# A retuned transformer block: first modulation in channel halves, first norm's inverse root on ScalarE

## The chip, the cores and the metric

The kernel runs as one program on one core of a Trainium2 chip. The metric is device time in microseconds (us). A core has five instruction streams that run side by side and meet only at semaphores: PE (TensorE, matmuls), ACT (ScalarE), DVE (VectorE), POOL (GpSimd) and SP (SyncE, which here only issues DMAs). A DMA is issued in an instant or, where its queue is full, in a few us, and lands much later.

## The reference

One block of an adaptive-layer-norm transformer, with 2048 tokens, 512 channels, 32 heads of 16 and a hidden width of 1792:

```python
mod = (silu(c) @ w_mod).reshape(1, 6, 1, 512)          # sa, ca, ga, sb, cb, gb
h = layernorm(x) * (1 + ca) + sa
q, k, v = split(h @ wqkv)                              # 32 heads of 16
# each token attends to itself and 7 earlier tokens, 2 apart
logits[s, w] = q[s] . k[s - 2 * w] * 16 ** -0.5        # w = 0..7, masked below token 0
x = x + ga * (softmax(logits) @ v) @ wo
h = layernorm(x) * (1 + cb) + sb
x = x + gb * ((gelu(h @ w_gate) * (h @ w_up)) @ w_down)
```

Shift `sa` and scale `1 + ca` are the first 1024 of the 3072 columns of `silu(c) @ w_mod`. Every channel of the first normalized activation needs its own two numbers from there, so the first q, k and v product waits for x, for c and for these columns.

## The kernel before, in words

Tokens go through in five groups (`GROUPS`): two of 256, then three of 512. For each group `ln1` (L567) normalizes rows, transposes them on PE and modulates them into `hT`; `emit_qkv` (L609) multiplies by wq, wk, wv and stores v to a scratch in DRAM; `emit_attention` (L657) reads v back as `vR`, forms the products on DVE (`pq`, `pv`), folds them on PE and ends in the output projection, the second norm and `h2T`; `emit_ffn` (L832) does gate, up and down products.

The order of instructions on each engine is not the order of the code. Every piece of work is an `Op` with an engine, an estimated duration and a priority; `Plan.order` (L92) places, again and again, the piece that could start earliest (start plus `MARGIN` of its engine), and among equals the one with the lowest priority number. `PRI`, `MARGIN`, `AHEAD` and `SKEW` (L200 to L219) are the knobs of that list. On the chip each engine then runs its list strictly in order. For loads: those with a priority under -996.9 are placed as soon as SP is free, the others no earlier than `AHEAD` us before the planned end of the transfers already issued. Buffers of one tag and sequence must be begun in the order in which they were made: x goes into `xs` in order, `wm2` can be loaded only after the tile `wide`, which needs `silu(c)`, has been placed, and the `qkv_ps` accumulators of group 0 come before those of group 1.

The first group, step by step. SP issues x of tokens 0 to 255 (L366), then `wm01`, the 1024 shift and scale columns, as one load with 2048 bytes in a row (L403), then wq, wk (L406), x of tokens 256 to 511, wv, more x. PE begins with 12 matmuls on zeros (L430), turns c into a column (L441) and does 4 more on zeros; ACT applies silu (L446). DVE takes the statistics of x (L578, L580), adds epsilon (L582); POOL raises to the power -1/2 (L513); DVE normalizes (L508); PE transposes both 128-token blocks (L553). `mod_first` (L469) multiplies `wm01` with silu(c) on PE, channel block 0 first and then blocks 1 to 3, both shift and scale, and adds 1 to the scale with a further one-column matmul (L483). DVE reads those numbers straight from PSUM to modulate the four channel blocks of `hT` (L561). q and k of the first half of the heads start block by block as `hT` arrives; order for this group: q, k, q, k, v, v. `mod_keep` (L489) copies shift and scale for the later groups. The other load names: `wm2` and `wm5` (gates ga, gb), `wm3` and `wm4` (shift and scale of the second norm), `woP`, `Wg`, `Wu`, `WdP`. `woP` and `WdP` are multiplied by the gates on DVE (L898, L901).

ACT holds one table of functions at a time. `emit` (L167) asks for the table with both exp and ln when the plan goes from a piece marked `silu` or `gelu` to one marked `exp`.

Of the kernel before, what the change touches and what calls it, by code (L numbers as in the profile page):

```python
# [184 lines left out]
class Engines:  # L185
    def __init__(self, nc, pl):
# [9 lines left out]
        ("rstd", 4), ("xn1", 2), ("xn2", 2), ("hT", 2), ("qT", 3), ("vT", 3), ("vR", 2), ("prod", 6), ("Lb", 1),  # L196
        ("e", 1), ("oT", 1), ("h2T", 2), ("gl", 3), ("ub", 3), ("hh", 8))
BLOCKS1 = ()
BLOCKS2 = ()
PRI = {  # L200
        "ln1": (-1549, -553.9, -424.8, -117.9, 420.6),
        "qkv": (-226.2, 479.5, 310.9, 823.2, 1490.9),
        "att": (-63.2, 258.1, -1202.2, 1315.4, 916.4),
        "ffn": (1214.3, 2234.3, 2417.5, 2391, 546),
        "glu": (-1006.6, 100.6, -1510.2, -71.4, 1415.7),
        "mod": (393, -373, -33.5),
        "wo": 1028.5,
        "wd": 1181.4,
        "scr": -3561.5,
        "vR": -3846.6,  # L210
        "warm": (12, 4, 0, 3),
        "load": {"wv": -989.49, "x1": -989.99, "x2": -962.38, "wm2": -989.49, "wo": -888.99, "x3": -991.49,
        "wm3": -899.52, "wm4": -990.99, "x4": -981.04, "Wg": -864.95, "Wu": -877.79, "wm5": -867.98, "Wd":
        -873.85},
}
Plan.MARGIN = {"pe": 0.34, "act": 1.25, "dve": 0.46, "pool": -1.19, "sp": 1.04}
Plan.AHEAD = 2.79
Plan.SKEW = 1.27
Plan.TURN = 0  # L219
# [3 lines left out]
def kernel(  # L223
# [13 lines left out]
    nc = tc.nc  # L237
# [44 lines left out]
    neghalf = ctile([P, 4], F32, "neghalf")  # L282
    onecol = ctile([P, 1], BF16, "onecol")
    M = ctile([P, H], BF16, "Mph")
    F1 = ctile([P, P], BF16, "F1")
# [23 lines left out]
    def consts_dve():  # L309
        nc.vector.memset(warm(), 0.0)  # L310
        nc.vector.memset(one1[:], 1.0)
        nc.vector.memset(neghalf[:], -0.5)
        nc.vector.memset(onecol[:], 1.0)

    def consts_ident():
# [27 lines left out]

    dve(0.6, consts_dve, w=[(early, 0), one1, neghalf, onecol], pri=-1000)
    gp(1.0, consts_ident, w=[ident], pri=-1000)
# [24 lines left out]

    wm01 = T("vR", [P, 4, 2 * D], BF16, "wm01", "early")
    wm3 = T("h2T", [P, 4, D], BF16, "wm3")
# [20 lines left out]
    def load_rows(t, src, p, cuts, late=0.0):  # L393
# [8 lines left out]
    load_x(0, 2, -1000)  # L402
    dma(1049e3, lambda: nc.sync.dma_start(out=wm01[:], in_=w_mod[:, 0:2 * D].rearrange("(t p) n -> p t n", p=P)),  # L403
        w=[wm01], pri=-999, bw=385e3)
    for b in range(3):
        dma(524e3, lambda b=b: nc.sync.dma_start(  # L406
            out=wqkv[b][:], in_=A_wqkv[:, b * D:(b + 1) * D].rearrange("(dt p) n -> p dt n", p=P)), w=[wqkv[b]],
            pri=(-998, -997, L["wv"])[b])
    load_x(2, 4, L["x1"])
# [58 lines left out]

    def mod_first(src, p):  # L469
        parts = []  # L470
        for chs in ((0,), (1, 2, 3)):
            n = len(chs)
            mps = T("psF", [P, 2 * n], F32, "modT_ps")

            def cols(chs=chs, n=n, mps=mps):
                for half in range(2):
                    for i, ch in enumerate(chs):
                        col = mps[:, half * n + i:half * n + i + 1]
                        for kt in range(4):
                            nc.tensor.matmul(col, lhsT=src[:, kt, half * D + ch * P:half * D + (ch + 1) * P],  # L480
                                             rhs=scT[:, kt:kt + 1], start=(kt == 0), stop=(kt == 3 and half == 0))
                        if half:
                            nc.tensor.matmul(col, lhsT=ident[:], rhs=onecol[:], start=False, stop=True)  # L483

            pe(0.25 * n, cols, r=[src, scT, ident, onecol], w=[mps], pri=p)
            parts.append((chs[0], n, mps))
        return parts

    def mod_keep(parts, p):  # L489
        for lo, n, mps in parts:  # L490
            act(0.2, lambda lo=lo, n=n, mps=mps: nc.scalar.copy(out=scl[:, lo:lo + n], in_=mps[:, n:2 * n]), r=[mps],
                w=[(scl, 0)], pri=p)
            act(0.2, lambda lo=lo, n=n, mps=mps: nc.scalar.copy(out=modT[:, lo:lo + n], in_=mps[:, 0:n]), r=[mps],
                w=[(modT, 0)], pri=p)
# [11 lines left out]

    def norm(tok, xn, i, mean, rstd, p):
        dve(0.325, lambda: nc.vector.tensor_scalar(  # L508
            out=xn[:, i, :], in0=xrow(tok), scalar1=mean[:, i:i + 1], scalar2=rstd[:, i:i + 1], op0=ALU.subtract,
            op1=ALU.mult), r=[xkey(tok), mean, rstd], w=[(xn, i)], pri=p)  # L510

# [3 lines left out]

    tp0 = []

# [25 lines left out]
    def transposed(xns, n, dst, off, p, seq, tags, split):  # L543
        per = 2 if n == SG else 4
        for dtp in range(DT // per):
            tp = T(tags[dtp], [P, per, n], BF16, "tp", seq)
            tp0.append(tp)
            for half, xn in enumerate(xns):
                def trans(half=half, dtp=dtp, tp=tp, xn=xn):
                    for i in range(2):  # L550
                        for dd in range(per):
                            dt, c4 = per * dtp + dd, 2 * half + i
                            nc.tensor.transpose(tp[:, dd, c4 * P:(c4 + 1) * P], xn[:, i, dt * P:(dt + 1) * P],  # L553
                                                ident[:])

                pe(0.115 * per, trans, r=[xn, ident], w=[(tp, half)], pri=p)
            for dd in range(per):
                dt = per * dtp + dd
                if split:
                    lo, nm, mps = mod0[min(dt, 1)]  # L560
                    dve(0.07 + n * 1.041e-3, lambda dt=dt, dd=dd, tp=tp, i=dt - lo, nm=nm, mps=mps: nc.vector.tensor_scalar(  # L561
                        out=dst[:, dt, 0:n], in0=tp[:, dd, 0:n], scalar1=mps[:, nm + i:nm + i + 1],
                        scalar2=mps[:, i:i + 1], op0=ALU.mult, op1=ALU.add), r=[tp, mps], w=[(dst, dt)], pri=p)
                else:
                    modulate(dst, lambda dd=dd, tp=tp: tp[:, dd, 0:n], dt, off, n, p, [tp])

    def ln1(g, dst, p):  # L567
        xns = []
        tok0, n = GROUPS[g]
        for half in range(n // 256):  # L570
            tok = tok0 + 256 * half
            st = T("st", [P, 2, 6], F32, "st", "ln1")
            mv = T("mv", [P, 2, 2], F32, "mv", "ln1")
            rstd = T("rstd", [P, 2], F32, "rstd", "ln1")
            xn = T("xn1", [P, 2, D], BF16, "xn", "ln1")
            xns.append(xn)
            for i in range(2):
                dve(0.6, lambda i=i, st=st, tok=tok: nc.vector.bn_stats(out=st[:, i, :], in_=xrow(tok + P * i)),  # L578
                    r=[xkey(tok + P * i)], w=[(st, i)], pri=p)
                dve(0.081, lambda i=i, st=st, mv=mv: nc.vector.bn_aggr(out=mv[:, i, :], in_=st[:, i, :]),  # L580
                    r=[(st, i)], w=[(mv, i)], pri=p)
            dve(0.09, lambda rstd=rstd, mv=mv: nc.vector.tensor_scalar_add(out=rstd[:], in0=mv[:, :, 1],  # L582
                                                                          scalar1=EPS), r=[mv], w=[rstd], pri=p)
            invsqrt(rstd, p)
            if g == 0:
                gp(2.4, consts_late, r=[ident, rstd], w=[NB, MA, MB], pri=-900)
            for i in range(2):
                norm(tok + P * i, xn, i, Mean(mv), rstd, p)
        if g in BLOCKS1:
            transposed_by_blocks(xns, dst, 0, p)  # L590
        else:
            transposed(xns, n, dst, 0, p, "ln1", ("psL",) if g == 0 else ("psF", "psF"), g == 0)

    class Mean(Tl):


        def __init__(self, mv):
            self.__dict__ = mv.__dict__

        def __getitem__(self, k):  # L600
# [8 lines left out]
    def emit_qkv(g):  # L609
# [3 lines left out]
        vs = [T("vT", [P, 2 * nj, HALO + n], BF16, "vT") for _ in range(2 // nj)]  # L613
        order = [(b, j) for j in range(0, 4, nj) for b in range(2)] + [(2, j) for j in range(0, 4, nj)]
        if g == 0:
            for t in vs:
                gp(0.2, lambda t=t: nc.gpsimd.memset(t[:, :, 0:HALO], 0.0), w=[(t, "halo")], pri=-800)
        for step, (b, j) in enumerate(order):
# [11 lines left out]
            if g == 0 and step < 2:  # L630
                for k, dt in enumerate(range(DT)):
                    pe(2 * 0.115, lambda b=b, j=j, ps=ps, dt=dt: mm(b, j, ps, range(nj), (dt,)),
                       r=[wqkv[b], (hT[g], dt)], w=[ps], pri=p + 0.01 * k, pad=ps if dt == 0 else None)
            else:
# [251 lines left out]

    mod0 = mod_first(wm01, -970)
    for g in range(NG):
# [48 lines left out]
```

## Time and profile before

| | us |
|---|---|
| median of 4 runs | 249.83 |
| lowest and highest | 248.35 and 252.61 |
| the profiled execution | 249.91 |
| its span in the profile | 247.7 |
| PE busy in the span | 240.4 (97%) |
| DVE busy, ACT busy | 159.2 (64%), 159.6 (64%) |
| POOL busy | 17.3 (7%) |
| PE idle, waiting for a transfer, in the whole span | 2.3 |

The profile cuts the span into 40 slices and gives the busy tenths of each engine; DMA is the busy share of the 16 DMA engines. A matmul's record is longer than the step from one to the next, because they overlap: eight 256-column or four 512-column matmuls take 0.87 us in a steady stretch of the chain, though each record says 273 or 379 ns. So a busy PE may still hold time in which nothing new is fed to it.

### The profile page before, as it was taken

Reading aid. Unit: us, or ns where it says so; the run is one execution under the profiler, and the core shown is the slowest. Engines: PE = TensorE matmul, PEld = TensorE weight load, DVE = VectorE, ACT = ScalarE, POOL = GpSimd, SP = SyncE. Lnnn points to the kernel's source line nnn. Section 1 sums busy time; section 2 is a strip of 40 time slices with the busy share of each in tenths; the row PEclk is TensorE's granted clock in tenths of the full one; section 3 lists DMA queues with packets and bytes.
Section 4 is the critical chain, followed back from the end, with each engine's and each line's share of the span. In section 5 each row is a group of like instructions: output and inputs, shape, how many; then the busy total and the mean of one; then the engine's idle time right before and its main releaser. Section 6 shows DMA issues by size and latency. Waiting matters only on the chain.

```text
span 247.7 us, 4324 instructions
## 1 busy us (share of the span) xinstructions
PE 240.4 (97%) x1669; PEld 130.5 (53%) x1669; DVE 159.2 (64%) x303; ACT 159.6 (64%) x289; POOL 17.3 (7%) x39
## 2 busy tenths in 40 slices
PE   7898999998999999999999999999999999999994
PEld 2786655556864547575444445443454444444453
DVE  3689937989996499982799983299552222222222
ACT  2287889689729779488777488936679501666400
POOL 5324020010001000020000011000110000000000
PEclk9999999999999999999999999999999999999999
DMA  6999999998530119800129400001000010100011
GB/s 218 360 368 326 280 251 274 269 318 188 131 57 0 45 46 238 148 0 4 44 64 190 92 0 0 22 22 44 0 4 0 0 39 6 42 0 0 3 42 42
DMA packets 25398, 25.88 MB, mean 104 GB/s; under 512 B 1313, under 2 KB 23714, under 8 KB 25378
## 3 DMA queue, kind: packets, MB, share of 16 engines
q1 hardware_dynamic: 25376, 25.61, 39.9%
q8 instruction: 13, 0.21, 0.4%
q14 instruction: 7, 0.06, 0.1%
q10 hardware_dynamic: 2, 0.00, 0.0%
HBM read 21.40 MB, written 4.21 MB: 103 GB/s over the span
## 4 chain that ended last, share of the span: by engine, by line
PE 77%; DMA 13%; SPq 5%; ACT 3%; issue 1%; DVE 0%; ACTq 0%
PE g_ps L847 20%; PE u_ps L847 20%; PE y_ps L873 20%; PE qkv_ps L626 5%; PE x_ps L806 5%; DMA Wg<-in_B_w_gate_dram 5%; DMA wm<-in_w_mod_dram 4%; DMA scr<-vT 3%; PE o_ps L782 3%; PE LT L701 2%; SPq L366 2%; PE tp L553 2%; ACT hT L519 2%; SPq L389 1%; SPq L406 1%
## 5 line engine op out<-in xcount | busy, mean ns | idle before, releaser
L847 PE MATMUL g_ps<-h2T,Wg 128*128 128x512 bf16 (+1 forms) x280 | 57.9, 337 | 1.1 <-DMA Wg<-in_B_w_gate_dram 1.1
L847 PE MATMUL u_ps<-h2T,Wu 128*128 128x512 bf16 (+1 forms) x280 | 57.6, 336 | 0.0
L856 ACT ACTIVATE gl<-g_ps 128x512 bf16<-128x512 f32 x56 | 33.6, 600 | 28.0 <-PE g_ps L847 19.1
L873 PE MATMUL y_ps<-WdP,hht 128*128 128x512 bf16 (+1 forms) x238 | 50.4, 367 | 0.0
L860 DVE TENSOR_TENSOR hht<-gl,ub 128x512 bf16<-128x512 bf16 x56 | 23.3, 422 | 37.5 <-ACT ub L859 37.3
L859 ACT CAST ub<-u_ps 128x512 bf16<-128x512 f32 x56 | 32.8, 586 | 14.8 <-PE u_ps L847 14.7
L847 PEld LDWEIGHTS <-Wg 128*128 128x128 bf16 x280 | 26.7, 98 | 24.8 <-issue 2.8
L847 PEld LDWEIGHTS <-Wu 128*128 128x128 bf16 x280 | 27.0, 98 | 20.8 <-issue 1.1
L691 DVE TENSOR_TENSOR pq<-qT,kT 128x2048 bf16<-128x2048 bf16 x32 | 37.7, 1217 | 0.0
L873 PEld LDWEIGHTS <-hht 128*128 128x128 bf16 x238 | 23.1, 98 | 25.0 <-issue 0.4
L766 DVE TENSOR_TENSOR pv<-e,vR 128x2048 bf16<-128x2048 bf16 x24 | 28.1, 1218 | 0.1
L881 DVE TENSOR_TENSOR x_sg<-y_ps,x_sg 128x512 bf16<-128x512 f32 (+1 forms) x17 | 10.6, 655 | 26.6 <-PE y_ps L873 26.6
L513 POOL TENSOR_TENSOR rstd<-rstd,neghalf 128x2 f32<-128x2 f32 x16 | 12.9, 811 | 164.3 <-DVE rstd L821 144.7
L626 PE MATMUL qkv_ps<-hT,wq 128*128 128x512 bf16 (+1 forms) x80 | 17.1, 337 | 0.5 <-DVE hT L561 0.3
L626 PE MATMUL qkv_ps<-hT,wk 128*128 128x512 bf16 (+1 forms) x80 | 16.7, 337 | 0.6 <-DMA wk<-in_A_wqkv_dram 0.4
L626 PE MATMUL qkv_ps<-hT,wv 128*128 128x512 bf16 (+1 forms) x80 | 15.5, 337 | 0.0
L806 PE MATMUL x_ps<-woP,oT 128*128 128x512 bf16 x64 | 15.3, 379 | 0.0
L813 ACT ACTIVATE xn<-x_sg 128x512 bf16<-128x512 bf16 x16 | 10.0, 630 | 6.3 <-DVE x_sg L810 6.1
L519 ACT ACTIVATE h2T<-tp,modT,scl 128x512 bf16<-128x512 bf16 (+1 forms) x20 | 12.2, 700 | 1.3 <-PE tp L553 1.3
L578 DVE BATCH_NORM_STATS2 st<-x_sg 128x6 f32<-128x512 bf16 x16 | 10.1, 682 | 3.5 <-DMA x_sg<-in_A_x_dram 3.5
L647 ACT CAST qT<-qkv_ps 128x512 bf16<-128x512 f32 x16 | 9.4, 596 | 3.6 <-PE qkv_ps L626 3.5
L810 DVE SCALAR_TENSOR_TENSOR x_sg<-x_ps,x_sg 128x512 bf16<-128x512 f32 x16 | 10.8, 685 | 1.4 <-PE x_ps L806 1.3
(89 smaller groups left out, 221.9 us busy)
## 6 DMA issues: line engine op xcount, KB each, us to landing
vR<-scr SPq DMA_DIRECT2D x24, 260.0 KB, 5.3
vR<-scr SPq DMA_DIRECT2D x8, 264.0 KB, 8.5
out_dram<-x_sg SPq DMA_DIRECT2D x15, 128.0 KB, 1.7
Wu<-in_B_w_up_dram SPq DMA_DIRECT2D x2, 896.0 KB, 10.0
scr<-vT SPq DMA_DIRECT2D x7, 256.0 KB, 7.1
WdP<-in_B_w_down_dram SPq DMA_DIRECT2D x2, 896.0 KB, 9.2
Wg<-in_B_w_gate_dram SPq DMA_DIRECT2D x2, 896.0 KB, 10.2
x_sg<-in_A_x_dram SPq DMA_DIRECT2D x3, 512.0 KB, 9.1
```

Of the source, the lines that this page charges most:

```text
L513: gp(0.75, lambda: nc.gpsimd.tensor_tensor(out=rstd[:], in0=rstd[:], in1=neghalf[:, 0:2], op=ALU.pow), r=[rstd, neghalf], w=[rstd], pri=p)
L519: act(act_us(n, 2), lambda: nc.scalar.activation(out=dst[:, dt, 0:n], in_=src(), func=ACT.Identity, scale=scl[:, off // 2 + dt:off // 2 + ...
L626: nc.tensor.matmul(ps[:, jl, :], lhsT=wqkv[b][:, dt, j + jl:D:4], rhs=columns(hT[g], dt, n, g in BLOCKS1), start=(dt == 0 and (jl == 0 or ...
L691: dve(1.145, lambda j=j, wg=wg, no=no, t=pq[m]: nc.vector.tensor_tensor(out=t[:], in0=_ap(q[g][:, j, :], [[0, no], [1, n]]), in1=_ap(kT[:, ...
L766: dve(1.145, lambda jj=jj, jl=jl, wg=wg, t=pv[m]: nc.vector.tensor_tensor(out=t[:], in0=_ap(e[:, wg, :], [[0, 4], [1, n]]), in1=vR[g][jj][ ...
L806: nc.tensor.matmul(x1_ps[:], lhsT=oT[:, j, c4 * P:(c4 + 1) * P], rhs=woP[:, j, :], start=(j == 0), stop=(j == 3))
L810: dve(0.69, lambda i=i, tok=tok, x1_ps=x1_ps, sx=sx: nc.vector.scalar_tensor_tensor(out=xrow(tok), in0=x1_ps[:], scalar=1.0, in1=xrow(tok) ...
L847: nc.tensor.matmul(ps[:, f, :], lhsT=Wt[:, dt, ft * P:(ft + 1) * P], rhs=columns(h2[g], dt, n, g in BLOCKS2), start=(dt == 0), stop=(dt == ...
L856: act(act_us(SG), lambda gl=gl, ps=gu[0]: nc.scalar.activation(out=gl[:], in_=flat(ps), func=ACT.Gelu_apprx_tanh), r=[gu[0]], w=[gl], pri= ...
L859: act(act_us(SG), lambda ub=ub, ps=gu[1]: nc.scalar.copy(out=ub[:], in_=flat(ps)), r=[gu[1]], w=[ub], pri=p)
L860: dve(0.339, lambda gl=gl, ub=ub, ht=hh[u // 2], u=u: nc.vector.tensor_tensor(out=ht[:, u % 2, :], in0=gl[:], in1=ub[:], op=ALU.mult), r=[ ...
L873: nc.tensor.matmul(y_ps[:], lhsT=hh[u // 2][:, u % 2, f * n + c4 * P:f * n + (c4 + 1) * P], rhs=WdP[:, ft, lo_d:hi_d], start=(ft == 0), st ...
```

## The change

The shift and scale columns are loaded as two tiles, one for channels 0 to 255 and one for 256 to 511, each by two loads (shift, scale) with 512 bytes in a row; the first half of wq is issued between the tiles, the second behind them. The small product that forms shift and scale goes in these halves, and it is placed in PE's order behind the transposes. In group 0 the transposes are cut by token block, and each waits for its own normalized rows. Epsilon and the inverse root of group 0 go, token block by token block, to ACT as `exp(-0.5 * ln(var + eps))`. The order of group 0's products becomes q, q, k, k, v, v, both q products accumulate as the channel blocks of `hT` arrive, and each matmul of them waits for its own rows of wq. The copies of shift and scale wait for the whole `hT`. The late constants on POOL no longer wait for the inverse root. All knobs of the plan have other values.

```diff
-        "load": {"wv": -989.49, "x1": -989.99, "x2": -962.38, "wm2": -989.49, "wo": -888.99, "x3": -991.49,
-        "wm3": -899.52, "wm4": -990.99, "x4": -981.04, "Wg": -864.95, "Wu": -877.79, "wm5": -867.98, "Wd":
-        -873.85},
+        "load": {"wv": -992.6, "x1": -995.05, "x2": -985.49, "wm2": -994.76, "wo": -873.3, "x3": -999.9, "wm3":
+        -873.8, "wm4": -870.88, "x4": -999.4, "Wg": -865.31, "Wu": -867.07, "wm5": -863.72, "Wd": -864.81},
-        "warm": (12, 4, 0, 3),
+        "warm": (5, 10, 0, 3),
...
-Plan.MARGIN = {"pe": 0.34, "act": 1.25, "dve": 0.46, "pool": -1.19, "sp": 1.04}
-Plan.AHEAD = 2.79
-Plan.SKEW = 1.27
+Plan.MARGIN = {"pe": 0.32, "act": 1.04, "dve": 0.26, "pool": 0.19, "sp": 0.56}
+Plan.AHEAD = 3.15
+Plan.SKEW = 0.49
...
-    wm01 = T("vR", [P, 4, 2 * D], BF16, "wm01", "early")
+    wm01 = [T("vR", [P, 4, 2, D // 2], BF16, "wm01", "early") for _ in range(2)]
...
-    dma(1049e3, lambda: nc.sync.dma_start(out=wm01[:], in_=w_mod[:, 0:2 * D].rearrange("(t p) n -> p t n", p=P)),
-        w=[wm01], pri=-999, bw=385e3)
+    def load_wm01(i):
+        for half in range(2):
+            lo = half * D + i * (D // 2)
+            dma(262e3, lambda half=half, lo=lo: nc.sync.dma_start(
+                out=wm01[i][:, :, half, :], in_=w_mod[:, lo:lo + D // 2].rearrange("(t p) n -> p t n", p=P)),
+                w=[(wm01[i], half)], pri=-999 + 0.5 * i + 0.1 * half, bw=385e3)
...
+    load_wm01(0)
+    load_wm01(1)
+    load_wqkv(0, -998.75, 2)
+    load_wqkv(1, -997)
+    load_wqkv(2, L["wv"])
...
-        for chs in ((0,), (1, 2, 3)):
+        for i2, chs in enumerate(((0, 1), (2, 3))):
...
-            pe(0.25 * n, cols, r=[src, scT, ident, onecol], w=[mps], pri=p)
+            pe(0.25 * n, cols, r=[src[i2], scT, ident, onecol] + after, w=[mps], pri=p)
...
+    def rsqrt_act(out_, in_):
+        nc.scalar.activation(out=out_, in_=in_, func=ACT.Ln, bias=eps1[:])
+        nc.scalar.activation(out=out_, in_=out_, func=ACT.Exp, scale=-0.5)
...
+                if split:
+                    for i in range(2):
+                        pe(0.0575 * per, lambda i=i, trans=trans: trans((i,)), r=[(xn, i), ident], w=[(tp, i)], pri=p)
...
+                if onact and g == 0:
+                    act(0.45, lambda mv=mv, rstd=rstd, i=i: rsqrt_act(rstd[:, i:i + 1], mv[:, i, 1:2]), r=[(mv, i), eps1],
+                        w=[(rstd, i)], pri=p, table="exp")
...
         if g == 0:
+            order = [(b, j) for b in range(3) for j in range(0, 4, nj)]
```

## The prediction

> **What bounds the kernel now.** I read the 40 slices first, then PE's waits, then the first 25 us instruction by instruction.
>
> ```profile
> PE   7898999998999999999999999999999999999994
> ACT  2287889689729779488777488936679501666400
> DMA  6999999998530119800129400001000010100011
> ```
>
> PE is full from the second slice on, the transfers fill their engines until about 60 us and are sparse after. To see what PE really feeds, I counted matmuls by shape in the groups of PE: 776 full ones of 512 columns at 0.216 us (four take 0.87), 352 of 256 at 0.109, 320 column-tiled ones that run four at a time (14), 128 transposes at 0.056 (7), and some one-column ones (2): 167.5 + 38.4 + 14 + 7 + 2 = 229 us. Of the span of 247.7 us, 19 us are therefore not work. Placing the same sums along the trace: 7.0 us go before the first transpose, 3.1 after the last matmul, about 5.6 are lost between 7 and 60 us, and 3 in the 185 us after, where none of PE's waits falls. They are few:
>
> ```profile
> PE warm_ps L430 <- DVE onecol L313: 1.3, 1, 1.3
> PE g_ps L847 <- DMA Wg<-in_B_w_gate_dram: 1.1, 1, 1.1
> PE modT_ps L458 <- DMA wm<-in_w_mod_dram: 0.8, 1, 0.8
> PE qkv_ps L626 <- DMA wk<-in_A_wqkv_dram: 0.4, 1, 0.4
> PE qkv_ps L626 <- ACT hT L519: 0.3, 2, 0.2
> PE qkv_ps L626 <- DVE hT L561: 0.3, 1, 0.3
> ```
>
> (Engine and line, what it waited for: us in total, times, longest.) So the change, which touches only the first 16 us and the order of the rest, can win a few us at most: PE's work is the same apart from one zero matmul less (12 + 4 become 5 + 10), and only lost time can go.
>
> **The inverse root.** The chain before, from the timeline (start, us, instruction, wait):
>
> ```profile
> 5.20 0.17 DVE L582 TENSOR_SCALAR rstd<-mv 128x2 f32<-128x2 f32 x1
> 5.46 0.70 POOL L513 TENSOR_TENSOR rstd<-rstd,neghalf 128x2 f32<-128x2 f32 x1 [1.95 <-DVE rstd L582]
> 6.13 1.04 PE L430 MATMUL warm_ps<-early 128*128 128x512 bf16 x4
> 6.20 0.73 DVE L508 TENSOR_SCALAR xn<-x_sg,mv,rstd 128x512 bf16<-128x512 bf16 x2 [0.83 <-POOL rstd L513]
> 7.00 0.61 PE L553 MATMUL tp<-ident,xn 128*128 128x128 bf16 x8
> 8.54 1.07 DVE L561 TENSOR_SCALAR hT<-tp,modT_ps 128x256 bf16<-128x256 bf16 x3 [0.27 <-PE modT_ps L483]
> ```
>
> Removed: 0.17 + 0.70 us and two hand-overs, from 5.17 to 6.20. Added: two ACT instructions per token block. The nearest rows are the one-column copies (0.16) and ln and exp on 256 columns (0.43, 0.37, less 0.21 for the columns): 0.16 to 0.22 each, about 0.4 a block. But ACT needs silu first, by my reading of the order rule (silu's input is ready before the variance), and then another table. c's landing isn't in the trace: it was issued at 0.80; x, 256 KB issued at 0.81, took 2.8 us to land, an output of 128 KB 1.7, so 2.5 to 3.6. PE's five zero matmuls end at about 3.4 (0.43 us each from 1.26), c's column takes 0.25, silu 0.17: about 4.1. The table:
>
> ```profile
> 33.65 0.58 ACT L647 CAST qT<-qkv_ps 128x512 bf16<-128x512 f32 x1 [0.28 <-PE qkv_ps L626]
> 34.25 1.28 ACT L254 ACT_TABLE_LOAD   x1
> 35.54 0.60 ACT L738 ACTIVATE e<-LT 128x512 bf16<-128x512 f32 x1
> ```
>
> A load shuts ACT for 1.3 us from one instruction's end to the next one's start, so it ends at 5.4, 0.2 after the first variance. The roots come at 5.85 and 6.25, the normalized blocks at 6.3 and 6.7 instead of 6.93 for both. The Trainium skill speaks against this: "ScalarE: Activation LUTs", section "What ACT_TABLE_LOAD costs", has 1.28 us for the load and 1.38 more for a drain. By that the blocks would come at 7.7 and 8.1, 1.2 later than before. The row above shows the load and no drain, so I go by the row.
>
> The transposes then wait for PE's ten zero matmuls instead: from 3.9, at 0.43 us until the step quickens at about 5.4 as it did before, then 0.216, to about 6.85. So PE is late next: **0.15 us gained**, not 0.4; and if the quickening comes one stretch later, up to 1.3 lost here. The shift and scale halves (18 one-column matmuls, about 0.5 us each) follow at 7.4 and 8.0; `hT` is complete at 9.4 against 9.61.
>
> The load of the exp table at 34.25 goes, since nothing needs another table in between: 1.28 us off ACT where it is busy 9.32 of 10 us (30 to 40 us) and where DVE sits idle 4.75 us for the softmax. Group 0's `h2T` then comes up to 1.28 earlier than 56.5. For PE this has no price of its own.
>
> **The loads.** One issue becomes four and another two, 4 more at 0.46 to 0.51 us, 2 us on SP. SP is ahead of the transfers, though: wk, the seventh load then, is issued by 4.8 and its 0.5 MB cannot begin before 8.2. So nothing, as long as the transfers are the limit. These rows (times to landing, last) give the rhythm:
>
> ```profile
> wq<-in_A_wqkv_dram SPq DMA_DIRECT2D x1, 512.0 KB, 6.4
> wk<-in_A_wqkv_dram SPq DMA_DIRECT2D x1, 512.0 KB, 7.4
> wv<-in_A_wqkv_dram SPq DMA_DIRECT2D x1, 512.0 KB, 8.3
> ```
>
> Issued at 1.81, 2.36 and 3.69, they land at 8.2, 9.75 and 12.0: 0.5 MB per 1.5 us, 349 GB/s. At this rate the channel halves land at 5.2 and 7.4 (needed at 7.4 and 8.0), wq at 8.2, wk at 9.75. The rows get shorter, however, 512 bytes for 2048. The nearest row is the reading back of v for the 256-token groups, 528 bytes in a row:
>
> ```profile
> 28.00:30.00 2.00, 2.00 (x40) 1.30 (x40) 2.00 (x7) 2.00 (x4) 0.00 (x0) 1.00 1.22 183
> 30.00:32.00 2.00, 2.00 (x13) 1.07 (x12) 1.55 (x6) 1.93 (x5) 1.02 (x2) 1.00 1.23 191
> ```
>
> (Last column GB/s.) At 190 GB/s the 1.05 MB would take 5.5 us instead of 3.0: **0 to 2.5 us** on everything behind. Those rows start at odd offsets and share the time with a write, the new ones do not, so I take the near end, 0.4. The skill's "DMA: Bandwidth & Descriptors", section "Specifications", names 512 bytes as the least transfer for full rate, which would make it 0; no row here has that size.
>
> **The q product and wv.** Before, PE had fed 4 of the 32 q and k matmuls when wk landed. With q first it can feed all 16 by about 10.0; k follows to 11.8. That would be 1.3 us ahead, but wv is late next: `wm2` now has a lower number than wv, and `wide` is placed in time, so its 0.5 MB go first. wv lands at 13.5 (13.9 with the 0.4), v ends 1.73 us later at 15.2 to 15.6; before, v ended at 15.24. Group 1's products cannot pass. Behind it PE fed three fillers (0.81 us) and waited for ACT's `hT`, so a few tenths there are free. The first 16 us: **-0.15 to +0.4, taken as +0.2.**
>
> **The end of the loads.** Before, Wu, Wd, wm5 and last Wg: the second half of Wg lands at 58.6, and PE loses 1.35 us before it. Now the numbers say Wu, Wg, Wd, wm5. Wg takes Wd's place, which landed at 39.8 and 43.3, so this wait goes: **-1.0 to -1.35**. Next in its place is `h2T`, by the table load earlier. Wd and its scaling (7 of 0.68 us on DVE, 53.0 to 57.3) move behind 58; the first down product is at 75.6, 18 us of cover. DVE is full from 60 to 70, so uncovered it would cost up to 4.8; PE has 8.63 us of qkv at 83.1 to move ahead. Fillers (0.8 us) and the wait for `wm3` (0.8) depend on the new order: they may go or double, -1.6 to +1.6 us. I take 0, since `wm3` and `wm4` still stand behind the same x and beside `woP`.
>
> Sum, against the profiled 249.91 (span 247.7 and 2.2 around it, 0.1 over the median): +0.2 - 1.1 = -0.9, **249.0 us**.
>
> **Rivals.**
> - *No gain.* PE has as much work as before, and the wait for Wg becomes one for `h2T` or for `wm3`: 249.9 + 0.2 = 250.1. For it: everything up to 60 us hangs on transfers that are full anyway. Against: PE, not the loads, has the longer sum.
> - *The lost time goes as a whole.* Wg 1.35, `wm3` 0.8, wk, `hT` and fillers 1.0: 246.8. For it: each is a wait of one transfer. Against: wv behind `wm2`.
> - *Short rows.* At 190 GB/s the second channel half lands near 9.7 and wv near 15.9, v ends at 17.6, 2.4 late; group 0's attention and `h2T` come as much later, so the gain at Wg goes too: 252.3. It decides from about 290 GB/s downwards, where the delay passes the 0.5 us of free fillers.
> - *The change doesn't do what it says:* the root comes no earlier, because PE's zero matmuls end after it. That is already in the 0.15; it costs 0.15.
>
> **Chances and range.** Forecast 0.45, no gain 0.2, all lost time 0.13, short rows 0.22. A measurement of this kernel tells about 1% (2.5 us) from nothing. Faster by over 1% (under 247.4): most of the third case, 0.12. Slower by over 1% (over 252.4): half of the last and a little of the second for a missed order, 0.15. Within: 0.73. The range takes the third case's figure below, 246.8, and above the last with part of a DVE hold-up, 252.9.
>
> **What would show it.** Right: a table load between silu and the first ln at about 4; first transposes near 6.9; wk at 9.8; PE idle or slow before wv at 13.5; no PE wait for Wg; no table load at 34. Wrong: zero matmuls past 8 us; channel halves landing after 8; a wait of PE after 60 us, where the new knobs were free to make one.

## The result, and the profile after

The changed kernel takes 251.6 us in the median of 43 runs, the one before 249.46 in the median of 64 beside it. The ratio is 1.005, with a 95% interval of 1.0032 to 1.0069: **about 1.25 us slower**. (The plain median is higher than the ratio makes it, because some executions in it were slow, nearly all of them while PE was granted a lower clock; the ratio leaves these out.) That is inside the predicted range and within 1%, but on the other side of zero from the forecast of 0.9 us faster.

The profiled execution shown here took 250.86 us with a span of 248.7, against 249.91 and 247.7 before. The 40 slices:

```profile
PE   7977999999999999999999999999999999999995
ACT  5265898899549669568987569825769501666400
DMA  6999999999800019800107900001000000100011
```

PE is full as before, except that slices 3 and 4 (12.4 to 24.9 us) show 7 where before they showed 9 and 8. PE's waits (engine and line, what it waited for: us in total, times, longest):

```profile
PE modT_ps L476 <- DMA wm<-in_w_mod_dram: 1.6, 2, 1.4
PE qkv_ps L665 <- DMA wv<-in_A_wqkv_dram: 1.5, 1, 1.5
PE warm_ps L448 <- DVE one L313: 1.3, 1, 1.3
PE mb_ps L519 <- DMA wm<-in_w_mod_dram: 0.4, 1, 0.4
PE qkv_ps L665 <- DMA wk<-in_A_wqkv_dram: 0.3, 1, 0.3
PE modT_ps L498 <- DMA wm<-in_w_mod_dram: 0.2, 1, 0.2
```

The wait for `Wg` of before is gone. New are a wait for `wv`, a longer one for `wm3` and `wm4` (L476), and one at L519, `mb_ps`: the product that forms the second gate, `gb`, from `wm5`.

To see where time went I made the same tally as for the prediction: at a time t, t minus the work that PE had been fed by then (each matmul at its step, zero matmuls counted as nothing). The work is 228.9 us in all kernels, so these columns can be subtracted, in us:

| lost until | before | after | after minus before |
|---|---|---|---|
| 7 | 6.9 | 6.9 | 0.0 |
| 15 | 7.8 | 9.7 | +1.9 |
| 22 | 9.3 | 9.9 | +0.6 |
| 24 | 10.2 | 11.5 | +1.2 |
| 30 | 10.3 | 12.0 | +1.7 |
| 57 | 11.1 | 12.7 | +1.6 |
| 60 | 12.5 | 12.8 | +0.3 |
| 65 | 12.5 | 13.6 | +1.2 |
| 240 | 15.4 | 16.5 | +1.1 |

The wait for `Wg` (57 to 60) was worth 1.3 us and went, as forecast. But 1.9 us came in the first 15 us. Of these 1.3 went back by 22 us, where the kernel before loses 1.5 on fillers (matmuls on `ident` that keep PE busy and whose result nobody uses) and on ACT's `hT`, and this one 0.2. Another 1.1 came between 22 and 30 us, at the products of `wm3` and `wm4`, and 0.9 between 60 and 65. After that nothing changes. The first 18 us on PE (start, us, instruction, wait):

```profile
3.69 3.84 PE L448 MATMUL warm_ps<-early 128*128 128x512 bf16 x10
7.37 0.61 PE L575 MATMUL tp<-ident,xn 128*128 128x128 bf16 x8
...
8.77 0.25 PE L498 MATMUL modT_ps<-scT,wm 128*128 128x1 bf16 x4 [0.15 <-DMA wm<-in_w_mod_dram]
...
9.03 1.92 PE L665 MATMUL qkv_ps<-hT,wq 128*128 128x256 bf16 x16
11.21 1.94 PE L665 MATMUL qkv_ps<-hT,wk 128*128 128x256 bf16 x16 [0.27 <-DMA wk<-in_A_wqkv_dram]
14.70 1.06 PE L665 MATMUL qkv_ps<-hT,wv 128*128 128x256 bf16 x8 [1.54 <-DMA wv<-in_A_wqkv_dram]
```

The last part of the shift and scale columns is multiplied at 8.77, k starts at 11.21 and v at 14.70: each stands behind a load that has just landed. The transfers in that stretch (1 us per row; the last three columns are the granted clock, the DMA share and GB/s), first the kernel before, then the changed one:

```profile
4.00:5.00 1.00, 1.00 (x3) 0.30 (x2) 1.00 (x4) 0.00 (x0) 0.00 (x0) 1.00 1.04 403
...
4.00:5.00 1.00, 1.00 (x4) 0.35 (x3) 1.00 (x4) 1.00 (x1) 0.79 (x5) 1.00 0.63 142
5.00:6.00 1.00, 1.00 (x4) 0.40 (x3) 0.58 (x3) 0.95 (x4) 0.57 (x3) 1.00 1.02 332
```

From 4 to 5 us only 142 GB/s are moved; before, the same stretch had 403. The landings, worked out from each issue and its time to landing, say the same: x 3.56, the four parts of `wm01` at 4.47, 6.51, 7.97 and 8.72, with wq's halves at 7.23 and 9.44. Before, all of `wm01` was there at 6.73 and wq at 8.24. Between the first part and the second lie 2.04 us, between each two after them 0.72 to 0.75.

### The profile page after: what moved, and what is told of

It is laid out like the page before. It is cut to its first block, busy times and chain, and to the rows that moved or that the text cites. A ratio compares the mean times of both kernels' runs of the same rounds, so it can differ in the third digit from the quotient of the medians.

```text
span 356.3 us, 4322 instructions
## 1 busy us (share of the span) xinstructions
PE 352.1 (99%) x1665; PEld 158.6 (45%) x1665; DVE 161.3 (45%) x303; ACT 165.3 (46%) x293; POOL 16.9 (5%) x38
## 4 chain that ended last, share of the span: by engine, by line
PE 99%; DVE 0%; issue 0%
PE y_ps L912 21%; PE u_ps L886 21%; PE g_ps L886 21%; PE qkv_ps L665 18%; PE x_ps L845 6%; PE o_ps L821 3%; PE LT L740 3%; PE tp L575 3%; PE warm_ps L448 2%; PE ss L785 1%; PE LT L770 1%; PE mb_ps L519 1%; PE modT_ps L498 0%; PE modT_ps L476 0%; DVE x_sg L920 0%; DVE early L312 0%
## 5 line engine op out<-in xcount | busy, mean ns | idle before, releaser
L886 PE MATMUL u_ps<-h2T,Wu 128*128 128x512 bf16 (+1 forms) x280 | 83.1, 447 | 0.0
L886 PE MATMUL g_ps<-h2T,Wg 128*128 128x512 bf16 (+1 forms) x280 | 82.9, 446 | 0.0
L912 PE MATMUL y_ps<-WdP,hht 128*128 128x512 bf16 (+1 forms) x238 | 76.6, 493 | 0.0
L886 PEld LDWEIGHTS <-Wu 128*128 128x128 bf16 x280 | 33.5, 122 | 40.0 <-issue 35.6
L665 PE MATMUL qkv_ps<-hT,wk 128*128 128x512 bf16 (+1 forms) x80 | 23.4, 441 | 0.0
L665 PE MATMUL qkv_ps<-hT,wv 128*128 128x512 bf16 (+1 forms) x80 | 22.6, 446 | 0.0
L845 PE MATMUL x_ps<-woP,oT 128*128 128x512 bf16 x64 | 22.5, 511 | 0.0
L849 DVE SCALAR_TENSOR_TENSOR x_sg<-x_ps,x_sg 128x512 bf16<-128x512 f32 x16 | 10.9, 690 | 13.6 <-PE x_ps L845 13.6
L665 PEld LDWEIGHTS <-wv 128*128 128x128 bf16 x80 | 10.3, 132 | 9.7 <-issue 8.6
L665 PEld LDWEIGHTS <-wk 128*128 128x128 bf16 x80 | 10.1, 128 | 9.7 <-issue 8.3
L852 ACT ACTIVATE xn<-x_sg 128x512 bf16<-128x512 bf16 x16 | 10.1, 630 | 9.5 <-DVE x_sg L849 9.5
L686 ACT CAST kT<-qkv_ps 128x512 bf16<-128x512 f32 x16 | 9.4, 588 | 10.7 <-PE qkv_ps L665 10.7
```

Of the source, the lines that this page charges most:

```text
L665: nc.tensor.matmul(ps[:, jl, :], lhsT=wqkv[b][:, dt, j + jl:D:4], rhs=columns(hT[g], dt, n, g in BLOCKS1), start=(dt == 0 and (jl == 0 or ...
L845: nc.tensor.matmul(x1_ps[:], lhsT=oT[:, j, c4 * P:(c4 + 1) * P], rhs=woP[:, j, :], start=(j == 0), stop=(j == 3))
L849: dve(0.69, lambda i=i, tok=tok, x1_ps=x1_ps, sx=sx: nc.vector.scalar_tensor_tensor(out=xrow(tok), in0=x1_ps[:], scalar=1.0, in1=xrow(tok) ...
L886: nc.tensor.matmul(ps[:, f, :], lhsT=Wt[:, dt, ft * P:(ft + 1) * P], rhs=columns(h2[g], dt, n, g in BLOCKS2), start=(dt == 0), stop=(dt == ...
L912: nc.tensor.matmul(y_ps[:], lhsT=hh[u // 2][:, u % 2, f * n + c4 * P:f * n + (c4 + 1) * P], rhs=WdP[:, ft, lo_d:hi_d], start=(ft == 0), st ...
```

## The experiments

Four theories stood for the first 16 us. Short rows: rows of 512 bytes are moved slowly. Order: `wm2` ahead of `wv` makes v late (the expectations call these two together the loads theory). Clock: PE runs its zero matmuls at the slow step of 0.43 us for longer, so the transposes come late. Knobs: the new numbers place work badly, whatever the loads do. After the first runs another took the place of the first: a **hole** of about 1.2 us that several small loads leave at the start of the queue. For 60 to 65 us the theory was that `wm5`, now the last of the loads, is late for its product. All ratios are against the kernel before, run on the same chip.

**The changed kernel again**, unedited, beside the next three.

> The changed kernel, for a profile of an undisturbed execution and a time beside the kernel before. All theories: about 1.2 us (0.5%) slower than before. Loads theory (512-byte rows, and wv behind wm2): the second channel half lands after 8 us, wv lands near 14.5 instead of 12.0, and PE waits for wv before group 0's v product, 1 us or more. Clock theory (PE stands still before the column of c, and the zero matmuls and what follows run at the slow step for longer): the step is 0.43 us beyond 5.4 us from the start and the transposes begin after 7.3. Knobs theory: the first 16 us cost nothing against before, and the time is lost between 16 and 60 us or after.

251.93 us against 249.2, ratio 1.0112 (1.0078 to 1.0145). The profile above is of this run. So the loss repeats, and on this chip it was twice the pooled one. The clock theory's sign is there: the zero matmuls step by 0.43 us until 6.66, and the transposes begin at 7.37.

**wv ahead of wm2.**

```diff
-        "load": {"wv": -992.6, "x1": -995.05, "x2": -985.49, "wm2": -994.76, "wo": -873.3, "x3": -999.9, "wm3":
+        "load": {"wv": -992.6, "x1": -995.05, "x2": -985.49, "wm2": -990.0, "wo": -873.3, "x3": -999.9, "wm3":
```

Only SP's list changes: wv is issued before the two loads of `wm2`.

> The changed kernel with one load moved: wv is issued ahead of wm2, as in the kernel before; every other engine's list is the same. Loads theory: wv lands 1.5 us earlier, the v product starts with no wait, 0.5 to 1.2 us faster than the changed kernel. Short-row theory alone: about 0.5 of that. Clock and knobs theories: no change beyond 0.3 us.

250.92 us, ratio 1.0078 (1.0037 to 1.0119). Better by 0.3% than the changed kernel beside it, but the intervals overlap. The order of wv is at most a part of it.

**One load of `wm01`.** The product stays in halves; the columns come in one tile and one load, 2048 bytes in a row, and wq's two halves behind it.

```diff
-    wm01 = [T("vR", [P, 4, 2, D // 2], BF16, "wm01", "early") for _ in range(2)]
+    wm01 = T("vR", [P, 4, 2 * D], BF16, "wm01", "early")
...
-    load_wm01(0)
-    load_wm01(1)
+    dma(1049e3, lambda: nc.sync.dma_start(out=wm01[:], in_=w_mod[:, 0:2 * D].rearrange("(t p) n -> p t n", p=P)),
+        w=[wm01], pri=-999, bw=385e3)
```

> The changed kernel with the 1024 shift and scale columns loaded in one tile by one load with 2048 bytes in a row, and wq's two parts behind it; the halves of the product and all other lists stay. Short-row theory: wk lands at 9.8 instead of 11, wv 1.0 to 1.4 earlier, and the kernel is 0.6 to 1.2 us faster than the changed one, as fast as before. If the rows cost nothing: 0 to 0.3 us slower, because the first channel half lands at 6.7 instead of 5.2. Clock and knobs theories: no change.

250.36 us, ratio 1.0037 (1.0008 to 1.0066) where the changed kernel beside it had 1.0112: some 1.9 us come back from the loads alone. The same second of transfers as above:

```profile
4.00:5.00 1.00, 1.00 (x4) 0.35 (x3) 1.00 (x4) 1.00 (x1) 0.79 (x5) 1.00 1.05 408
```

408 GB/s in place of 142. All of `wm01` has landed at 6.80, wk at 9.83, wv at 13.36, and the tally at 15 us falls from 9.7 to 8.3. PE's waits:

```profile
PE qkv_ps L658 <- DMA wv<-in_A_wqkv_dram: 1.2, 1, 1.2
PE modT_ps L469 <- DMA wm<-in_w_mod_dram: 1.1, 1, 1.1
...
PE mb_ps L512 <- DMA wm<-in_w_mod_dram: 0.5, 1, 0.5
```

v still waits, since `wm2` is still ahead of it, and `mb_ps` still waits. So the loads are a cause, but whether by the length of the rows or by the number of loads this run can't say: it changes both.

**The new code with the old order numbers.** All numbers of `PRI`, `MARGIN`, `AHEAD` and `SKEW` and the zero matmuls are those of before; the shift and scale product, which had no number then, gets -970.

```diff
-        "mod0": 282.8,
+        "mod0": -970,
...
-        "warm": (5, 10, 0, 3),
+        "warm": (12, 4, 0, 3),
...
-Plan.AHEAD = 3.15
-Plan.SKEW = 0.49
+Plan.AHEAD = 2.79
+Plan.SKEW = 1.27
```

> The changed code with all knobs of the kernel before (priorities, margins, zero matmuls 12 and 4) and the shift and scale product at the old priority -970. Knobs theory: 0.8 to 1.2 us faster than the changed kernel, as before. Loads theory: wv comes first here too, short rows stay: 0.3 to 0.8 faster. Clock theory: 12 zero matmuls leave no gap, but silu and with it the second table come 2 us later, so the root comes at about 8.3: slower in the first 10 us by 1.5.

251.18 us, ratio 1.01 (1.0054 to 1.0147). As slow as with the new numbers. Its four small loads land at 4.41, 6.33, 7.83 and 8.57: the hole is there too. With `wv` in its old place v starts at 13.09 after a wait of 0.3, so at 15 us the tally is only 8.1; but 2.9 go by 22 us, eight fillers (1.7 us) and a wait of 0.6 for ACT among them, and at 57 it stands at 13.3, against 12.7 with the new numbers. So the old numbers don't mend it: the new code loses as much with them, in other places.

**wm5 ahead of Wd.** Every engine's order is kept as the changed kernel has it, and the two loads of `wm5` alone are moved in SP's list.

```diff
         placed = self.order()
+        for ops, before in self.moves:
+            placed = [o for o in placed if o not in ops]
+            at = placed.index(before)
+            placed[at:at] = list(ops)
...
-    load_wm_halves(wm5, 5, L["wm5"])
-    load_rows(WdP, B_w_down, L["Wd"], 2)
+    gate2 = load_wm_halves(wm5, 5, L["wm5"])
+    down = load_rows(WdP, B_w_down, L["Wd"], 2)
+    pl.moves = [(gate2, down[0])]
```

> The changed kernel with the two loads of wm5 (the second gate) moved ahead of the two of Wd in SP's list; the lists of the other engines stay as they are. If the wait of PE at the second gate's product costs time (0.4 us in the profile of the changed kernel, 3.3 in that of the run with wv first): wm5 lands 5 us earlier, that wait is gone, 0.4 to 1.0 us faster than the changed kernel and a narrower spread of times. If that wait only takes up time that PE would lose later anyway: no change.

249.59 us against 249.19, ratio 1.0017 (0.9999 to 1.0034). `wm5` lands at 49.4 and 50.1 in place of 62.7 and 63.3, and `mb_ps` is gone from PE's waits:

```profile
PE qkv_ps L670 <- DMA wv<-in_A_wqkv_dram: 1.5, 1, 1.5
PE warm_ps L453 <- DVE one L319: 1.3, 1, 1.3
PE modT_ps L503 <- DMA wm<-in_w_mod_dram: 1.1, 2, 0.7
PE LT L745 <- DVE pq L735: 0.8, 1, 0.8
```

Between 60 and 65 us 0.1 is lost, not 0.9. The start is as bad as ever (wv 1.5, tally at 15 us 9.7), although the zero matmuls quicken at 4.91 here and the transposes begin at 6.42: PE waits 0.69 and 0.39 us for the columns instead, and k starts at 11.17 as it did at 11.21. So the clock theory isn't what costs the start. The median is about 1.5 us under those of the next two runs on the same chip, which keep `wm5` last: more than the 0.4 us of waiting in the profile above. The other profiles say how that wait varies: 0.5 us with one load of `wm01`, 2.6 and 1.3 in the next two runs.

**Four loads with long rows.** Four loads of 256 KB at the same places in SP's list, but each holds 128 rows of `w_mod` whole, 2048 bytes in a row.

```diff
-            lo = half * D + i * (D // 2)
-            dma(262e3, lambda half=half, lo=lo: nc.sync.dma_start(
-                out=wm01[i][:, :, half, :], in_=w_mod[:, lo:lo + D // 2].rearrange("(t p) n -> p t n", p=P)),
-                w=[(wm01[i], half)], pri=-999 + 0.5 * i + 0.1 * half, bw=385e3)
+            k = 2 * i + half
+            dma(262e3, lambda k=k: nc.sync.dma_start(
+                out=wm01[:, k, :], in_=w_mod[k * P:(k + 1) * P, 0:2 * D]),
+                w=[(wm01, k)], pri=-999 + 0.5 * i + 0.1 * half, bw=385e3)
```

> The changed kernel with the shift and scale columns still loaded by four loads of 256 KB at the same four places of SP's list, but cut by rows of w_mod, so with 2048 bytes in a row. If the short rows make the hole between the landing of the first and second part (2.0 us for 0.25 MB in the changed kernel): the parts land 0.7 to 0.8 us apart, the last by about 8.0 instead of 8.7, and wk by 9.9 instead of 11. If the number of loads makes it: the hole stays.

251.06 us, ratio 1.0076 (1.0045 to 1.0107), not the time of one load. The same stretch of the transfers:

```profile
4.00:5.00 1.00, 1.00 (x5) 0.39 (x4) 1.00 (x5) 1.00 (x1) 0.79 (x5) 1.00 0.78 213
```

The parts land at 4.11, 6.43, 7.77 and 8.41: 2.3 us from the first to the second, with rows four times as long. **The rows are not the cause; that the load comes in four small ones is.** The cost of short rows can be seen at most in the bits after the hole (0.64 to 0.70 us a part against 0.72 to 0.75). PE's waits in this run:

```profile
PE mb_ps L519 <- DMA wm<-in_w_mod_dram: 2.6, 2, 2.3
...
PE modT_ps L498 <- DMA wm<-in_w_mod_dram: 1.1, 2, 0.6
PE qkv_ps L665 <- DMA wv<-in_A_wqkv_dram: 1.0, 1, 1.0
```

Here the wait for `wm5` is the largest of all, 2.6 us, and the tally goes from 11.3 at 60 us to 14.3 at 65, while at 57 us this run was 1.4 better off than the changed kernel.

**The root of the first norm back on DVE and POOL.** Lists, loads and the table load stay; the two instructions of a block change engine.

```diff
-        nc.scalar.activation(out=out_, in_=in_, func=ACT.Ln, bias=eps1[:])
-        nc.scalar.activation(out=out_, in_=out_, func=ACT.Exp, scale=-0.5)
+        nc.vector.tensor_scalar_add(out=out_, in0=in_, scalar1=EPS)
+        nc.gpsimd.tensor_tensor(out=out_, in0=out_, in1=neghalf[:, 0:1], op=ALU.pow)
```

> The changed kernel with group 0's root computed as in the kernel before, epsilon added on DVE and the power -1/2 on POOL, but for each token block by itself; the lists and the table load stay where they are, only the four ACT instructions are replaced by two on DVE and two on POOL. By the step of the prediction (PE's zero matmuls end after the root): the first block is not later than PE, the second is normalized at about 7.3 instead of 6.7, transposes end 0 to 0.4 us later, and behind the wait for wv nothing of it is left: within 0.2 us of the changed kernel. If the root on ACT is worth something by itself: 0.5 or more slower.

251.22 us, ratio 1.0076 (1.0047 to 1.0105), beside 1.005 (1.0032 to 1.0069) of the changed kernel, which was not run on this chip, and the same 1.0076 of the four loads with long rows, which was: no difference that can be told. The second block's transposes come at 7.41, but the second half of the columns lands at 8.11 and 8.86 here, so the root isn't what PE waits for.

**The loads mended.** The changed kernel with one load of `wm01`, wv ahead of `wm2`, `wm4` ahead of `woP`, `wm5` ahead of Wd. Nothing of the rest is touched: the root is on ACT, the product in halves. The edits for wv, `wm01` and `wm5` come together, and one move more is made in SP's list:

```diff
-        "load": {"wv": -992.6, "x1": -995.05, "x2": -985.49, "wm2": -994.76, "wo": -873.3, "x3": -999.9, "wm3":
+        "load": {"wv": -992.6, "x1": -995.05, "x2": -985.49, "wm2": -990.0, "wo": -873.3, "x3": -999.9, "wm3":
...
-    load_wm01(0)
-    load_wm01(1)
+    dma(1049e3, lambda: nc.sync.dma_start(out=wm01[:], in_=w_mod[:, 0:2 * D].rearrange("(t p) n -> p t n", p=P)),
+        w=[wm01], pri=-999, bw=385e3)
...
+    pl.moves = [(gate2, down[0]), ([scale2], out_w[0])]
```

(`scale2` is the load of `wm4`, `out_w` those of `woP`.)

> The changed kernel with four repairs of SP's list alone: shift and scale in one load with 2048 bytes in a row, wv ahead of wm2, wm4 ahead of woP, wm5 ahead of Wd. Loads theory: PE's waits for wk, wv, wm4 and wm5 (0.3, 1.5, 1.4 and 0.4 us) go or shrink; 1.5 to 3 us faster than the changed kernel, so 0 to 1.5 us faster than the kernel before, and no wait for Wg. Knobs theory (the time is lost in the orders of the other engines): it stays 0.5 or more slower than before.

**248.44 us, ratio 0.9975 (0.9959 to 0.9991): faster than both kernels.** PE's waits, all that this view lists:

```profile
PE warm_ps L447 <- DVE one L319: 1.3, 1, 1.3
PE LT L739 <- DVE pq L729: 0.9, 1, 0.9
PE tp L574 <- DVE xn L526: 0.5, 1, 0.5
PE g_ps L885 <- ACT gl L894: 0.4, 1, 0.4
PE qkv_ps L664 <- DMA wv<-in_A_wqkv_dram: 0.3, 1, 0.3
```

Only 0.3 us of waiting for a transfer is left. Against the run with `wm5` moved alone, on the same chip, the other three moves are worth 1.15 us. The tally is 7.9 at 15 us, 10.5 at 57, 10.8 at 65 and 13.9 at 240, where before had 15.4: of the 19 us not fed, 1.5 went.

**wm5 ahead of Wd and one load of `wm01`, no more**: the two edits shown above together, wv behind `wm2` as in the change.

> As gate_early (wm5 ahead of Wd), and shift and scale in one load of 1 MB. With the wait at the second gate gone, what the hole costs should show by itself: wk and wv land 1.2 us earlier, PE's wait for wv shrinks from 1.5 to 1.2 or less and k starts 1.2 us earlier: 0.5 to 1.0 us faster than gate_early, ratio to the kernel before about 0.998. If the hole is covered by later waits: as gate_early, 1.0017.

248.87 us against 249.64, ratio 0.9986 (0.996 to 1.0012): level with before. With the hole (the run with `wm5` alone, on another chip) it was 1.0017, so the hole would be worth about 0.3% with the tail mended; but those two intervals overlap, so this pair alone doesn't show it. Nor does it tell what the moves of wv and `wm4` add: with them it was 0.9975. In its profiled execution, 1 us slower than the median, `wm01` landed only at 8.78, though 381 GB/s were moved from 4 to 5 us: one load can be late too, without the hole.

**The mended loads with the root on DVE and POOL**: the edit of the root and that of the loads together.

> As loads_mended, with group 0's root on DVE and POOL (one power a token block) in place of ACT's ln and exp. Here no transfer stands behind the transposes until wk at 9.9, and the shift and scale product starts at once when they end. If the root on ACT is worth its 0.4 to 0.7 us there: the ratio to the kernel before rises from 0.9975 to about 0.9995. If wk (9.9) and wv (12.1) take it back: 0.9975 to 0.998.

249.06 us, ratio 0.997 (0.9945 to 0.9996), against 0.9975 with the root on ACT. The root's place is worth nothing that can be measured, with the loads mended too.

**Two loads of 512 KB**, 2048 bytes in a row, wq's first half between them: half the number of pieces.

```diff
+        dma(524e3, lambda: nc.sync.dma_start(
+            out=wm01[:, 2 * i:2 * i + 2, :],
+            in_=w_mod[2 * i * P:(2 * i + 2) * P, 0:2 * D].rearrange("(t p) n -> p t n", p=P)),
+            w=[(wm01, 2 * i), (wm01, 2 * i + 1)], pri=-999 + 0.5 * i, bw=385e3)
```

> The changed kernel with shift and scale in two loads of 512 KB with 2048 bytes in a row, around the first part of wq. If the hole belongs to loads of 256 KB at the start of the queue, the first part lands at about 5.2 and the second, behind wq's first, at 7.5; if any cut makes it, the part after the first again lands 1.3 us late, so the second near 8.5 and wk at 11.

Inconclusive: two executions only, 248.87 and 254.12. In the profiled one, the longer, the parts land at 5.18 and 8.16 with wq's half at 5.93 between: 2.2 us from wq's half to the next part of 512 KB, which takes 1.5 at the usual rate. At 4 to 6 us it moved 366 and 316 GB/s. If that is the hole, it is smaller here; one profile doesn't settle it.

## Why the prediction was right or wrong

**The bound** held. PE's work is 228.9 us in every kernel, only lost time moved, and from 65 us on all kernels lose the same (2.8 to 3.1 us in the profiles tallied).

**The inverse root** went as predicted, on ACT (start, us, instruction, wait):

```profile
3.80 0.17 ACT L464 ACTIVATE scT<-c_ps 128x4 bf16<-128x4 f32 x1 [1.17 <-PE c_ps L459]
3.99 1.28 ACT L255 ACT_TABLE_LOAD   x1
5.29 0.29 ACT L536 ACTIVATE rstd<-mv,eps 128x1 f32<-128x1 f32 x1
5.61 0.20 ACT L537 ACTIVATE rstd<-rstd 128x1 f32<-128x1 f32 x1
5.72 0.28 ACT L536 ACTIVATE rstd<-mv,eps 128x1 f32<-128x1 f32 x1
6.03 0.20 ACT L537 ACTIVATE rstd<-rstd 128x1 f32<-128x1 f32 x1
```

Silu, then the table load near 4, roots at 5.81 and 6.23 (predicted 5.85 and 6.25). Ln is dearer than the 0.16 to 0.22 of the nearest rows, 0.29, and exp is not, 0.20; the second ln begins 0.09 before the first exp has ended. The Trainium skill's page "ScalarE: Activation LUTs", section "What ACT_TABLE_LOAD costs", counts 1.38 us more for a drain; here ln starts 1.30 us after the load starts, so there is no drain to see, and going by the row was right. "So PE is late next" was right too: the step of the ten zero matmuls quickened at 6.66 and not at 5.4, so the transposes started at 7.37 (predicted 6.85 to 6.9, before 7.00) though the blocks were ready from 6.3 on. The 0.4 lost there costs nothing, since the last of the columns came later still, at 8.72. The two runs without the root on ACT agree: its place is worth nothing that they can measure.

**The table load at 34** went. Group 0's first gate product starts at 56.07, where before it started at 57.18 and then waited for `Wg`.

**The loads, where the step failed.** "0 to 2.5 us on everything behind ... I take the near end, 0.4", and from that "the first 16 us: -0.15 to +0.4, taken as +0.2". It was +1.9 at 15 us. The columns and all behind them came about 1.2 us later: counting out wq's half that lies between, the last part landed at 8.0 where one load lands at 6.8, and k's products began at 11.21 behind wk, which I had at 10.15. The reason was not the one in the step. The rows of 512 bytes ran at full rate once the hole was passed: 0.25 MB in 0.74 us, some 350 GB/s, which agrees with the Trainium skill's page "DMA: Bandwidth & Descriptors", section "Specifications" (512 bytes is the least transfer for full rate). Of the two reasons given against the row at 190 GB/s one was misread: no packet of the write (512 bytes each) starts between 28 and 32 us there, they begin after 32. What cost time was that 1 MB came as four loads at the start of the queue. I had priced SP's four issues (2 us, rightly free: wk, the eighth load and not the seventh, was issued at 4.52) and the bytes, and never a gap between small loads, for which the trace of before had no row: its only load of 256 KB at the queue's start was x itself. The range of that step would have held 1.2; the mistake was to choose its near end for a reason about rows.

The rival "short rows" had the place, the sign and the chain (second half after 8 us, wv after 14, v late), with landings of 8.7 and 14.65 for its 9.7 and 15.9. Its mechanism fell with the four long-rowed loads, and its price of +2.4 us, 252.3, was too high. Its sign to look for, halves landing after 8 us, is the one that came true. The rival "no gain" was right that the wait for Wg becomes another one, but it named `h2T` or `wm3` for it, and not wm5; its 250.1 stands against 251.2, the profiled 249.91 times the ratio.

**wv behind wm2** was right in kind: 13.5 to 13.9 was predicted, 13.36 is what it is without the hole, 14.65 with it. The delay stops PE for 1.54 us before v, where group 1's work cannot pass, as the step itself said; without the hole it still waits 1.2. The "few tenths" of fillers said to be free behind it were in fact 1.3 us, so most of this came back by 22 us.

**The end of the loads** was half right. "Wg takes Wd's place ... so this wait goes: -1.0 to -1.35" measured -1.3 (tally, 57 to 60). Wd's scaling moved to 74.3 to 81.4 on DVE and PE's first down product starts at 77.47 without a wait, so that cover held. But "next in its place is `h2T`" was wrong. I wrote down the new order, "Wu, Wg, Wd, wm5", and followed Wg and Wd to who needs them, but not wm5. PE forms the second gate from it, at 62 us in the new order:

```profile
61.31 1.04 PE L886 MATMUL g_ps<-h2T,Wg 128*128 128x256 bf16 x8
62.72 1.23 PE L519 MATMUL mb_ps<-wm,wide 128*128 128x512 bf16 x4 [0.37 <-DMA wm<-in_w_mod_dram]
```

PE runs its list in order, so what stands behind this product waits with it. wm5 lands at 62.67 and 63.31, and in the tallied profiles that have it last PE waits 0.4 to 2.6 us for it: the wait that had gone is back under another name. The last line of the prediction, "a wait of PE after 60 us", was the sign to look for.

**Fillers and `wm3`** were taken as 0 within -1.6 to +1.6. The reason, that both loads still stand beside `woP`, holds for `wm3` alone: `wm4` was issued ahead of `woP` before (10.85, landing at 20.89) and stands behind it now (17.46, landing at 26.44). Between 15 and 30 us the profiled execution came out 0.2 better than before, 1.3 won on fillers and 1.1 lost on waits of 1.4 and 0.25 for `wm3` and `wm4`. But that stretch differs from one execution to the next, with the same order and the same hole. The tally of more runs shows it:

| lost until | 15 | 22 | 30 | 57 | 60 | 65 |
|---|---|---|---|---|---|---|
| before | 7.8 | 9.3 | 10.3 | 11.1 | 12.5 | 12.5 |
| changed kernel | 9.7 | 9.9 | 12.0 | 12.7 | 12.8 | 13.6 |
| `wm5` ahead of Wd | 9.7 | 9.8 | 11.2 | 11.7 | 11.8 | 11.9 |
| four loads, long rows | 9.1 | 9.3 | 10.7 | 11.3 | 11.3 | 14.3 |
| root on DVE and POOL | 9.7 | 9.8 | 12.4 | 13.4 | 13.3 | 14.9 |
| one load of `wm01` | 8.3 | 9.6 | 10.5 | 11.1 | 11.1 | 12.2 |
| loads mended | 7.9 | 8.1 | 10.1 | 10.5 | 10.6 | 10.8 |

The four rows with the hole are at 11.3 to 13.4 by 57 us, 12.3 in the mean, and the row of one load is at 11.1, as before. So I put the hole's late start at some 1.2 us by then, in one execution almost nothing and in another 2.3. That is an estimate with a single row of one load to hold on to; the medians give 1.9 us (one load against the changed kernel on the same chip) and 0.8 (the same with `wm5` moved, two chips, overlapping intervals).

The sum, as these rows give it: +1.2 for the start (mine: +0.2), -1.3 for `Wg` (mine: -1.1), and for `wm5`, which had no term, +0.9, +3.0, +1.6 and +1.1 in the four rows that have it last, 1.65 in the mean. That is about +1.5 us; the ratio says +1.25, the profiled pair +0.95. Which loads PE waits for is shown by the runs; how the loss divides among them is this estimate.

## What to carry to other kernels

Count the loads as well as the bytes when a transfer is cut at the head of a queue: four loads of 256 KB delivered the same 1 MB about 1.2 us later than one did. When a load is moved forward, follow whatever moved behind it to its own consumer and that consumer's place in the in-order list; a wait that goes may come back under the name of the transfer that is now last. And a shorter chain on one engine (the root) was worth nothing that could be measured here, while the products behind it waited for data by another way.

## What the runs showed of the hardware

- **A hole after the first small load.** In all six profiles with `wm01` in four loads of 256 KB, the first lands 0.6 to 0.9 us after x, the second 1.9 to 2.3 us after the first, the rest 0.64 to 0.78 apart (once 1.07), and 87 to 213 GB/s are moved from 4 to 5 us. In all five profiles with one load of 1 MB that stretch moved 381 to 408, and the load landed at 6.73 to 7.18 in four of them, at 8.78 in the fifth. It doesn't depend on the length of the rows (512 or 2048 bytes). Its mechanism wasn't found; whether it goes by the size of a load, by how many are in the queue, or by what else uses the queue's start is open.
- **The zero matmuls' end varies.** The ten of 512 columns began at 3.7 in both the profile above and that of the mended loads; their step went from 0.43 to 0.22 us at 6.66 in the one and at 4.86 in the other, and what followed them started at 7.37 and 6.37, with a granted clock of 1.00 in both. So the first transposes move by 1 us between executions of the same ten instructions.
- **The wait for the load that is last in a full queue varies**: with the first of `wm5`'s two loads issued at 52.08 and at 52.09 us, PE waited 0.4 us for them in the profile of the changed kernel and 2.6 in that of the four loads with long rows.
